# Values without their ones columns, loaded ahead of the second unit's queries and keys

## The chip, the cores and the metric

The kernel runs on one core of one Trainium2 chip. The metric is device time in microseconds (us); lower is better. Five engines take part: PE (TensorE, matrix products), DVE (VectorE), ACT (ScalarE), POOL (GpSimd) and SP (SyncE), which here only issues DMAs. Each runs its own queue strictly in order and meets the others at semaphores.

## The reference

The reference chains three layers. The change touches the first, a linear attention over 4 batches x 8 heads, 576 positions, head width 64, with 128 random features:

```python
q_p, k_p = (phi(q_s), phi(k_s))            # exp(projection - |x|^2/2 - max), 128 features
kv = np.einsum('bhsm,bhsd->bhmd', k_p, v)
z = np.sum(k_p, axis=2)
num = np.einsum('bhsm,bhmd->bhsd', q_p, kv)
den = np.einsum('bhsm,bhm->bhs', q_p, z)[..., None] + 1e-06
return (num / den).astype(np.float32)
```

A gated two-layer network of 2304 tokens (512 to 1536 to 512), the "MoE" of the code, and a soft mixture of 8 experts with 32 slots follow. Both are left as they are.

## The kernel before

**Units.** Attention goes in 16 units u of two heads each. A unit loads its transposed queries and keys (`QKTs`, from `qkT`), the same rows untransposed for the norms (`TOK`, from `tok`) and its values (`Vs`, from `von`). `chunk_proj` projects a piece of keys or queries on PE (K0, K1 and T for keys and tails, Q0 and Q1 for queries), DVE adds the norm and takes the minimum, ACT takes exponentials into `HKs`, `HTs` and `HQs`. `chunk_kv` multiplies the key features by the values, five matmuls for each head. `chunk_qT` transposes the query features, and `chunk_num` forms numerators and denominators, ACT and DVE divide, and the result goes into `XT`, the input of the next layer.

**The ones.** One matmul gives kv and z together: beside each 64 value columns stand 64 columns of ones (zero in the padded half of the fifth tile), values left for head 0 and right for head 1. Before, those constants lie in HBM inside `von` and come with each load: 640 KB per unit, 5120 contiguous bytes in each partition.

**Numerators in units 0 to 7.** There the numerator and the denominator of a half (288 positions) are four matmuls of 64 output rows, listed as `64x288`: denominator head 0, denominator head 1, numerator head 0, numerator head 1. Head 0 uses one half of the array's columns, head 1 the other.

**Order.** Nothing is written in program order. `Plan` records every operation with its reads and writes, a due time and a cost, `schedule` plays a list scheduler over all engines, and `issue` (L411) emits the result. For an overlap `span` takes the whole stretch from the first to the last element of an access, so a strided view stands for all that lies between. A change of one cost or dependency near the start can so reorder every engine for a long way. Matmuls of the MoE (`ga` gate, `va` value, `o` down) are due beside units 3 and on and fill PE. All of the trace's instructions carry line L411, so tiles tell them apart: `g_80` in an operand is `HKs`/`HQs`/`KVF` memory, `g1b` that of odd units, `g_78` the transposed inputs and `TOK`, `g_79` the values, `QTF` and the projection matrix.

Of the kernel before, what the change touches and what calls it, by code (L numbers as in the profile page):

```python
# [22 lines left out]
NT = 5  # L23
# [394 lines left out]
def body(ctx, tc, nc, qkT, tok, von, omT, wall, phi, w1, w2, ident_d, srep_d, rrep_d, mask_d, out):  # L418
    plan = Plan(nc)
    PE, ACT, DVE, POOL, SP = (Eng(plan, e) for e in ("PE", "ACT", "DVE", "POOL", "SP"))  # L420
# [54 lines left out]
    def region(k, dtype):  # L475
        return T([128, 4096], f"g{k}", dtype)
# [4 lines left out]
    def carve(reg, at, shape):  # L481
        n = int(np.prod(shape))
        names = "abcde"[:len(shape)]
        v = reg[:, at:at + n]
        if len(shape) == 1:
            return v
        return v.rearrange(f"p ({' '.join(names)}) -> p {' '.join(names)}",
                           **{c: d for c, d in zip(names, shape)})

    q0, q1, q2 = region(0, F32), half_region(0, F32), half_region(1, F32)  # L490
    g2, g3, g4 = (region(k, F32) for k in (2, 3, 4))
# [10 lines left out]

    QKTs = [carve(g2, 1152 * k, [1152]) for k in range(2)]
    TOK = carve(g2, 2304, [9, 2, D])
    Vs = [carve(g3, 1280 * k, [NT, 2, 128]) for k in range(2)]
    QTF = carve(g3, 2560, [2, S])
    obf = carve(g3, 3712, [256])
    HKs = [carve(r, 0, [4, 2, M]) for r in (g4, q2)]
# [17 lines left out]
    def bank(tag=None):  # L526
        if tag is None:
            tag = turn(FLW, "fl") if wide[0] else "fl"
        tag = "fl" if tag in POOLED else tag
        return plan.tile(psp, [128, 512], F32, tag, NFL if tag == "fl" else 1, dyn=tag == "fl")  # L530


    def load_unit(u):
        if u < NU:
            SP.dma_start(out=QKTs[u % 2], in_=qkT[u])
            SP.dma_start(out=Vs[u % 2], in_=von[u])
            SP.dma_start(out=TOK, in_=tok[u])

    def prep_qk(u, kind):
# [23 lines left out]
    def chunk_proj(u, i):  # L563

        if u >= NU:
            return
        c0, nt, hb, t0, g0 = PARTS[i]
        hb = hb[u % 2][:, t0:t0 + nt]
        x = QKTs[u % 2][:, c0:c0 + 128 * nt]
        if nt < 4:  # L570
            both = bank()[:, 0:256 * nt].rearrange("p (t h m) -> p t h m", h=2, m=M)
            ps = [both[:, :, h] for h in range(2)]
        else:
            ps = [bank()[:, 0:128 * nt].rearrange("p (t m) -> p t m", m=M) for _ in range(2)]

        def products():
            for t in range(nt):
                if nt < 4:
                    PE.matmul(both[:, t].rearrange("p h m -> p (h m)"), x[:, 128 * t:128 * t + 128], obf,
                              start=True, stop=True)  # L580
                    continue
                for h in range(2):
                    r = slice(64 * h, 64 * h + 64)
                    PE.matmul(ps[h][:, t], x[r, 128 * t:128 * t + 128], obf[r, 128 * h:128 * h + 128],
                              start=True, stop=True)

        plan.together(products, [SQ[:, g0:g0 + 2 * nt]], [hb])
        low = turn(MX, "mx")
        for h in range(2):
            for t in range(nt):  # L590
                g = 2 * t + h
                DVE.tensor_tensor_reduce(out=hb[:, t, h], in0=ps[h][:, t],
                                         in1=SQ[:, g0 + g:g0 + g + 1].to_broadcast([128, M]),
                                         scale=1.0 / 16.0, scalar=BIG, op0=ALU.add, op1=ALU.min,
                                         accum_out=low[:, g:g + 1])
        for h in range(2):
            for t in range(nt):
                g = 2 * t + h
                ACT.activation(out=hb[:, t, h], in_=hb[:, t, h], func=AF.Exp, scale=-1.0, bias=low[:, g:g + 1])

    def chunk_kv(u):

        ps = bank()[:, 0:256].rearrange("p (h c) -> p h c", h=2)
        for h in range(2):
            for t in range(NT):
                k = HKs[u % 2][:, t, h, :] if t < 4 else HTs[u % 2][:, 0, h, :]
                PE.matmul(ps[:, h, :], k, Vs[u % 2][:, t, h, :], start=t == 0, stop=t == NT - 1)
        if u < N_NUM:
            ACT.activation(out=KVF, in_=ps, func=AF.Copy, scale=1.0 / M)
            return  # L610
        ACT.activation(out=KV[:, 0], in_=ps, func=AF.Copy, scale=1.0 / M)
        DVE.scalar_tensor_tensor(out=KV[:, 1], in0=ps, scalar=1.0 / M, in1=KV[:, 0].bitcast(F32),
                                 op0=ALU.mult, op1=ALU.subtract)
# [552 lines left out]
    SP.dma_start(out=QKTs[0][:, 256:640], in_=qkT[0][:, 256:640])  # L1166
    SP.dma_start(out=QKTs[0][:, 640:1152], in_=qkT[0][:, 640:1152])
    SP.dma_start(out=TOK[:, 5:9], in_=tok[0][:, 5:9])
    SP.dma_start(out=QKTs[1], in_=qkT[1])
    SP.dma_start(out=Vs[0], in_=von[0])  # L1170
    SP.dma_start(out=ident, in_=ident_d)
    DVE.memset(one_b, 1.0)
    DVE.memset(den_b, 1e-6)
    DVE.tensor_scalar(out=obf, in0=obf, scalar1=-16.0 * float(D ** -0.25), scalar2=None, op0=ALU.mult)
# [4 lines left out]
    chunk_proj(0, "K1")  # L1179
    chunk_proj(0, "T")  # L1180
    SP.dma_start(out=TOK, in_=tok[1])
    SP.dma_start(out=Vs[1], in_=von[1])
    chunk_proj(0, "Q0")
    chunk_proj(0, "Q1")
    prep_qk(1, 0)
# [6 lines left out]
    start = START  # L1192
# [124 lines left out]
def layout(q, k, v, omega, moe_w_gate, moe_w_val, moe_w_out, moe2_phi, moe2_w1, moe2_w2):  # L1317
    def headsT(x):
        return x.reshape(B, H // 2, 2, S, D).transpose(0, 1, 2, 4, 3).reshape(NU, 128, S)

    def tiles(x, n):
        return x.reshape(NU, 2, n, 128, D).transpose(0, 3, 2, 1, 4)

    def pairs(x):
        return x.reshape(NU, 2, S, D)

    kT, qT = headsT(k), headsT(q)
    kp, qp, vp = pairs(k), pairs(q), pairs(v)
    tail = np.concatenate([kp[:, :, 512:], qp[:, :, 512:]], axis=2)
    vtail = tiles(np.concatenate([vp, np.zeros_like(vp[:, :, :64])], axis=2), NT)  # L1330
    ones = np.ones_like(vtail[:, :, :, 0])
    ones[:, 64:, NT - 1] = 0.0

    def up(w):
        return w.reshape(4, 128, NF, 128).transpose(2, 1, 0, 3).reshape(NF, 128, 512)

    f32 = np.float32
    p = np.arange(128)
    w2 = moe2_w2.reshape(E, 8, 128, DM).transpose(0, 2, 1, 3)
    big = np.finfo(f32).max  # L1340
    a = {
        "qkT": np.concatenate([kT, qT[:, :, 512:], qT[:, :, :512]], axis=2),
        "tok": np.concatenate([tiles(kp[:, :, :512], 4), tiles(tail, 1), tiles(qp[:, :, :512], 4)], axis=2),
        "von": np.stack([np.concatenate([vtail[:, :, :, 0], ones], axis=3),
                         np.concatenate([ones, vtail[:, :, :, 1]], axis=3)], axis=3),
        "omT": np.concatenate([omega.T, omega.T], axis=0),
        "wall": np.stack([up(moe_w_gate), up(moe_w_val), moe_w_out.reshape(NF, 128, DM)], axis=1).view(np.int64),
        "phi": moe2_phi.reshape(4, 128, NSLOT).transpose(1, 0, 2),
        "w1": moe2_w1.reshape(E, 4, 128, F).transpose(0, 2, 1, 3).reshape(E, 128, 4 * F),
        "w2": np.stack([x.reshape(E, 128, 2 * DM) for x in (w2[:, :, :4, :256], w2[:, :, 4:, :256],  # L1350
                                                            w2[:, :, :, 256:384], w2[:, :, :, 384:])], axis=1),
        "ident": np.eye(128, dtype=f32),
        "srep": (p[:, None] % 32 == np.arange(32)[None, :]).astype(f32),
        "rrep": (p[:, None] % 32 == p[None, :] % 32).astype(f32),
        "mask": np.where((p[:, None] % 32) // SPE == np.arange(E)[None, :], big, f32(0)).astype(f32),
    }
    return {f"in_{n}": np.ascontiguousarray(x) for n, x in a.items()}


def build(nc, arrays):  # L1360
    args = [nc.dram_tensor(n, a.shape, mybir.dt.from_np(a.dtype), kind="ExternalInput").ap()
            for n, a in arrays.items()]
    args.append(nc.dram_tensor("out_0", (NTOK, DM), F32, kind="ExternalOutput").ap())
    with tile.TileContext(nc, schedule_with_timeline_sim=True) as tc:
        with ExitStack() as ctx:
            body(ctx, tc, nc, *args)
# [8 lines left out]
```

## Time and profile before

| what | value |
|---|---|
| time, median of 3 runs | 684.1 us (683.9 to 684.46) |
| profiled execution, its own time | 683.73 us |
| span of that execution | 680.9 us |
| PE busy | 662.8 us |
| DVE, ACT, POOL busy | 442.4, 428.6, 283.7 us |
| DMA moved | 139.50 MB |

The span is what the trace shows of instructions; 2.83 us of the execution's own time lie outside it. Matmul ends are modelled and neighbours overlap in the trace, so the distance between starts tells more of PE than its busy time. An fp32 matmul has two records, an fp32r matmul or a transpose one.

### The profile page before, as it was taken

The page shows a single profiled execution, that of the slowest core. Times are in us where ns is not written, and L with a number is a line of the kernel's source. Part 1 is how long each engine was busy: PE and PEld are TensorE (multiplying, and loading weights), DVE is VectorE, ACT ScalarE, POOL GpSimd, SP SyncE. Part 2 cuts the span into 40 slices and gives each one's busy share as a digit, 9 for nine tenths or more (in the row PEclk, how much of TensorE's full clock was granted, in tenths as well). Part 3 has the DMA queues.
Part 4 walks back from the last instruction along what each step waited for, and adds up shares of the span by engine and source line. Part 5 has one row for each costly group of instructions (what it writes and reads, how often), then busy time and mean ns, then how long its engine had stood idle before and what let it go on. Part 6 is the DMA issues. An engine that isn't in the chain of part 4 may idle for free.

```text
span 680.9 us, 12655 instructions
## 1 busy us (share of the span) xinstructions
PE 662.8 (97%) x4404; PEld 534.2 (78%) x4404; DVE 442.4 (65%) x1306; ACT 428.6 (63%) x967; POOL 283.7 (42%) x245
## 2 busy tenths in 40 slices
PE   7999999999999999999999999999999999999995
PEld 6676777778888888887888888788888789899663
DVE  3899999899997476576566564566444335656423
ACT  5899898888887765756567675464444444675012
POOL 0465445465444443244444543444444444553100
PEclk9999999999999999999999999999999999999998
DMA  7889776787875345424353312689533238666988
GB/s 284 302 277 331 279 250 227 248 269 246 313 247 173 118 154 201 147 85 154 95 190 119 94 47 94 197 301 332 175 92 94 93 107 271 202 208 206 400 336 237
DMA packets 52494, 139.50 MB, mean 205 GB/s; under 512 B 5584, under 2 KB 13520, under 8 KB 52432
## 3 DMA queue, kind: packets, MB, share of 16 engines
q1 hardware_dynamic: 46624, 121.35, 53.0%
q10 hardware_dynamic: 5808, 17.37, 7.4%
q8 instruction: 34, 0.56, 0.3%
q14 instruction: 28, 0.23, 0.1%
HBM read 124.54 MB, written 14.16 MB: 204 GB/s over the span
## 4 chain that ended last, share of the span: by engine, by line
PE 86%; DMA 4%; DVE 3%; ACT 3%; issue 1%; SPq 1%; POOL 1%; DVEq 0%; POOLq 0%; ACTq 0%
PE o L411 25%; PE ga L411 22%; PE va L411 21%; PE fl L411 17%; DVE g L411 2%; DMA ws<-wscr 2%; ACT g L411 1%; DMA g<-in_von 1%; DMA g<-in_tok 1%; ACT ga_a L411 1%; SPq L411 1%; DMA wscr<-x 1%; DVE x2T L411 1%; POOL w L411 0%; POOL g L411 0%
## 5 line engine op out<-in xcount | busy, mean ns | idle before, releaser
L411 POOL TENSOR_TENSOR w<-ws,w 128x512 fp32r<-128x512 f32 x138 | 181.7, 1317 | 246.6 <-ACT w L411 114.3
L411 PE MATMUL ga<-XT,w 128*128 128x512 f32 (+1 forms) x720 | 168.4, 377 | 2.0 <-DVE ga_a L411 1.7
L411 PE MATMUL va<-XT,w 128*128 128x512 f32 (+1 forms) x720 | 167.3, 376 | 0.4 <-DVE ga_a L411 0.4
L411 PE MATMUL o<-gt,w 128*128 128x512 f32 (+1 forms) x720 | 167.5, 377 | 0.1
L411 PEld LDWEIGHTS ga<-XT,w 128*128 128x128 f32 x720 | 123.6, 189 | 27.2 <-DVE ga_a L411 2.6
L411 PEld LDWEIGHTS va<-XT,w 128*128 128x128 f32 x720 | 123.9, 189 | 25.9 <-issue 4.1
L411 PEld LDWEIGHTS o<-gt,w 128*128 128x128 f32 x720 | 123.6, 189 | 25.6 <-issue 3.9
L411 ACT ACTIVATE w<-ws 128x512 fp32r<-128x512 f32 x107 | 67.2, 628 | 61.1 <-PE o L411 19.5
L411 PE MATMUL fl<-g,g 64*128 64x128 f32 (+4 forms) x686 | 83.1, 313 | 3.2 <-DMA g<-in_qkT 1.4
L411 ACT ACTIVATE g<-g 128x128 f32<-128x128 f32 (+3 forms) x204 | 73.3, 410 | 13.9 <-DVE g L411 8.8
L411 ACT ACTIVATE ga_a<-ga_a 128x512 f32<-128x512 f32 (+1 forms) x120 | 69.9, 583 | 18.6 <-DVE ga_a L411 17.6
L411 PEld LDWEIGHTS fl<-g,g 64*128 64x128 f32 (+2 forms) x686 | 60.9, 183 | 23.7 <-issue 6.1
L411 ACT ACTIVATE ga_a<-ga 128x512 f32<-128x512 f32 (+1 forms) x60 | 33.2, 554 | 67.0 <-PE ga L411 66.9
L411 DVE SCALAR_TENSOR_TENSOR ga_a<-ga,ga_a 128x512 f32<-128x512 f32 (+1 forms) x60 | 38.0, 633 | 41.9 <-ACT ga_a L411 41.8
L411 DVE CAST w<-ws 128x512 fp32r<-128x512 f32 x55 | 23.5, 428 | 61.3 <-PE ga L411 41.6
L411 DVE TENSOR_TENSOR ga_a<-va,ga_a 128x512 f32<-128x512 f32 (+1 forms) x60 | 38.0, 634 | 17.7 <-ACT ga_a L411 12.5
L411 ACT ACTIVATE x2T<-g 128x512 f32<-128x512 f32 x72 | 45.4, 664 | 4.1 <-DVE x L411 4.1
L411 ACT ACTIVATE g1b<-g1b,g 128x128 f32<-128x128 f32 x128 | 40.4, 388 | 6.1 <-DVE g L411 6.1
L411 ACT ACTIVATE ga_a<-ga_a,one_b 128x512 f32<-128x512 f32 (+1 forms) x60 | 40.7, 679 | 1.4
L411 DVE TENSOR_SCALAR x2T<-x2T 128x512 f32<-128x512 f32 (+1 forms) x72 | 39.7, 564 | 2.8 <-ACT x2T L411 2.7
L411 DVE TENSOR_TENSOR g<-fl,g 64x288 f32<-64x288 f32 (+3 forms) x61 | 29.4, 484 | 17.8 <-ACT g L411 16.1
L411 POOL TENSOR_TENSOR XT<-g,XT 128x64 fp32r<-128x64 f32 (+2 forms) x43 | 28.6, 681 | 23.7 <-ACT ga_a L411 6.7
(197 smaller groups left out, 798.8 us busy)
## 6 DMA issues: line engine op xcount, KB each, us to landing
ws<-wscr SPq DMA_DIRECT2D x42, 512.0 KB, 3.6
ws<-wscr SPq DMA_DIRECT2D x78, 256.0 KB, 2.7
g<-in_wall SPq DMA_DIRECT2D x36, 512.0 KB, 4.9
g<-in_von SPq DMA_DIRECT2D x16, 640.0 KB, 5.7
wscr<-x SPq DMA_DIRECT2D x36, 256.0 KB, 4.8
g<-in_qkT SPq DMA_DIRECT2D x15, 576.0 KB, 5.1
g<-in_tok SPq DMA_DIRECT2D x15, 576.0 KB, 5.0
g<-in_w ACTq DMA_DIRECT2D x16, 512.0 KB, 5.5
```

What stands on the lines that cost most here:

```text
L411: ins = getattr(self.eng[e], method)(*a, **k)
```

## The change

The host layout drops the ones, so `von` holds 320 KB per unit, 2560 contiguous bytes per partition. In SBUF a unit's values are now three blocks of 5 x 64 columns: head 0, ones, head 1. The load writes blocks 0 and 2 (`0::2`, two runs of 1280 bytes in each partition), and DVE writes block 1 of both buffers once. The matmul of `chunk_kv` reads its 128 columns as two runs of 64, `h:h + 2`. The first value load now stands ahead of the second unit's `qkT`.

```diff
-    Vs = [carve(g3, 1280 * k, [NT, 2, 128]) for k in range(2)]
+    Vs = [carve(g3, 1280 * k, [3, NT, 64]) for k in range(2)]
...
-            SP.dma_start(out=Vs[u % 2], in_=von[u])
+            SP.dma_start(out=Vs[u % 2][:, 0::2], in_=von[u])
...
-                PE.matmul(ps[:, h, :], k, Vs[u % 2][:, t, h, :], start=t == 0, stop=t == NT - 1)
+                PE.matmul(ps[:, h, :].rearrange("p (a c) -> p a c", a=2), k, Vs[u % 2][:, h:h + 2, t, :],
+                          start=t == 0, stop=t == NT - 1)
...
+    SP.dma_start(out=Vs[0][:, 0::2], in_=von[0])
     SP.dma_start(out=QKTs[1], in_=qkT[1])
-    SP.dma_start(out=Vs[0], in_=von[0])
     SP.dma_start(out=ident, in_=ident_d)
+    for y in Vs:
+        DVE.memset(y[:, 1], 1.0)
+        DVE.memset(y[64:128, 1, NT - 1], 0.0)
...
-    SP.dma_start(out=Vs[1], in_=von[1])
+    SP.dma_start(out=Vs[1][:, 0::2], in_=von[1])
...
-        "von": np.stack([np.concatenate([vtail[:, :, :, 0], ones], axis=3),
-                         np.concatenate([ones, vtail[:, :, :, 1]], axis=3)], axis=3),
+        "von": vtail.transpose(0, 1, 3, 2, 4),
```

The scheduler turns this into another order on every engine. PE's order differs up to about a third of its list and is the same from there to the end. Three places follow.

PE, the first unit. Before, the two query projections of unit 0 (`fl<-g_79,g_78`, `o_87`) stand ahead of all ten kv matmuls (`o_88`):

```order
L411 MATMUL o_85<-g_79,g_78 128x256
L411 MATMUL fl<-g_79,g_78 128x256 x2
L411 MATMUL o_87<-g_79,g_78 128x256 x2
L411 MATMUL o_88<-g_79,g_80 128x128 x10
L411 MATMUL o_90<-ident,g_80 128x128 x4
```

In the changed kernel the same stretch reads:

```order
L411 MATMUL o_85<-g_79,g_78 128x256
L411 MATMUL o_88<-g_79,g_80 128x128 x5
L411 MATMUL fl<-g_79,g_78 128x256 x2
L411 MATMUL o_87<-g_79,g_78 128x256 x2
L411 MATMUL o_88<-g_79,g_80 128x128 x5
L411 MATMUL o_90<-ident,g_80 128x128 x4
```

Head 0's five kv matmuls, which need the values, moved ahead of the query projections, which do not.

PE, a little later: numerators of unit 0 (`64x288`) among projections of unit 1 (`128x256`). Before:

```order
L411 MATMUL fl<-g_79,g_80 64x288 x2
L411 MATMUL o_96<-g_79,g_80 64x288 x2
L411 MATMUL fl<-g_79,g_80 64x288 x2
L411 MATMUL fl<-g_79,g_78 128x256 x2
L411 MATMUL o_91<-g_79,g_78 128x256 x2
L411 MATMUL o_94<-g_79,g_78 128x256
L411 MATMUL o_100<-g_79,g_80 64x288 x2
```

In the changed kernel:

```order
L411 MATMUL fl<-g_79,g_80 64x288
L411 MATMUL o_96<-g_79,g_80 64x288
L411 MATMUL fl<-g_79,g_78 128x256 x2
L411 MATMUL o_91<-g_79,g_78 128x256 x2
L411 MATMUL o_94<-g_79,g_78 128x256
L411 MATMUL fl<-g_79,g_80 64x288
L411 MATMUL o_96<-g_79,g_80 64x288
L411 MATMUL fl<-g_79,g_80 64x288 x2
```

Head 0's denominator and numerator now stand alone ahead of the projections, and head 1's follow behind them; before, the two heads of each came together.

PE in unit 4, among MoE matmuls (`va`, `o` with `gt`, `ga`). Before:

```order
L411 MATMUL fl<-g_79,g_80 64x288 x4
L411 MATMUL va<-XT,w_152 128x512 x3
L411 MATMUL o_175<-gt,w_157 128x512
L411 MATMUL fl<-g_79,g_80 64x288 x2
L411 MATMUL o_175<-gt,w_157 128x512 x2
```

In the changed kernel:

```order
L411 MATMUL o_174<-gt,w_157 128x512 x2
L411 MATMUL fl<-g_79,g_80 64x288
L411 MATMUL o_174<-gt,w_157 128x512
L411 MATMUL o_175<-gt,w_157 128x512 x3
L411 MATMUL o_176<-gt,w_157 128x512 x3
L411 MATMUL fl<-g_79,g_80 64x288 x5
```

One matmul of a pair moved ahead of seven MoE matmuls, and the next five numerator and denominator matmuls stand together behind them.

## Rows read from the trace of the kernel before

**Rows 1.** Page, part 1: busy us (share of the span) and instructions of each engine.

```profile
PE 662.8 (97%) x4404; PEld 534.2 (78%) x4404; DVE 442.4 (65%) x1306; ACT 428.6 (63%) x967; POOL 283.7 (42%) x245
```

**Rows 2.** Chain of waits that ended last: start us, us, what it was.

```profile
4.53 0.43 SPq L411
...
5.00 0.43 SPq L411
...
5.48 7.99 DMA g<-in_von
...
13.60 2.92 PE o L411 x24
...
64.94 2.10 PE ga L411 x8
```

**Rows 3.** Windows: stretch, its length, engines' busy us (instructions), clock, DMA share, GB/s.

```profile
25.00:45.00 20.00, 18.37 (x118) 14.24 (x117) 19.05 (x89) 17.46 (x52) 12.69 (x13) 1.00 0.83 267
45.00:65.00 20.00, 18.78 (x134) 13.74 (x132) 18.67 (x77) 19.08 (x55) 10.79 (x12) 1.00 0.92 320
65.00:100.00 35.00, 35.00 (x220) 24.73 (x221) 33.41 (x108) 31.81 (x77) 15.40 (x14) 1.00 0.75 257
```

**Rows 4.** Timeline of PE, start: start us, us, operation, shapes, records [idle before].

```profile
7.34 2.77 PE L411 MATMUL o<-g,g 128*128 128x256 f32 x6
9.90 1.25 PE L411 MATMUL fl<-g,g 128*128 128x256 f32 x4
10.99 1.03 PE L411 MATMUL o<-g,g 128*128 128x256 f32 x4
13.60 2.47 PE L411 MATMUL o<-g,g 128*128 128x128 f32 x20 [1.58 <-DMA g<-in_von]
...
17.68 0.71 PE L411 MATMUL fl<-g,g 128*64 128x288 f32 x4 [0.52 <-ACT g L411]
18.22 0.66 PE L411 MATMUL o<-g,g 128*64 128x288 f32 x4
18.70 1.72 PE L411 MATMUL fl<-g,g 128*64 128x288 f32 x8
...
23.08 1.97 PE L411 MATMUL o<-g,g 128*128 128x256 f32 x8
24.88 0.61 PE L411 MATMUL fl<-g,g1b 128*128 128x128 f32 x4
```

**Rows 5.** DMAs issued from 4.6 to 7.5 us: count, size, us to landing.

```profile
g<-in_qkT SPq DMA_DIRECT2D x1, 576.0 KB, 6.9
g<-in_tok SPq DMA_DIRECT2D x1, 256.0 KB, 5.5
```

**Rows 6.** Timeline of DVE and ACT, 0 to 22 us.

```profile
0.86 0.64 DVE L411 MEMSET g<- 128x256 f32 x3 [0.86 <-PEq L1370]
...
9.63 1.86 ACT L411 ACTIVATE g<-g 128x128 f32<-128x128 f32 x6 [0.43 <-DVE g L411]
...
12.05 0.29 DVE L411 CUSTOM_DVE_ANT_0 g<-fl,g 128x128 f32<-128x128 f32 x1
...
12.39 2.45 ACT L411 ACTIVATE g<-g 128x128 f32<-128x128 f32 x8 [0.89 <-DVE g L411]
...
18.06 0.82 DVE L411 TENSOR_REDUCE g<-g 128x10 f32<-128x640 f32 x1 [4.23 <-POOL g L411]
...
21.17 0.28 DVE L411 CUSTOM_DVE_ANT_0 g1b<-fl,g 128x128 f32<-128x128 f32 x1
```

**Rows 7.** Timeline of PE, 50 to 81 us: numerators (128*64) among MoE matmuls.

```profile
53.04 0.70 PE L411 MATMUL o<-g,g 128*64 128x288 f32 x2
...
75.59 0.40 PE L411 MATMUL o<-gt,w 128*128 128x512 f32 x1
75.92 0.71 PE L411 MATMUL fl<-g,g 128*64 128x288 f32 x4
76.55 1.42 PE L411 MATMUL o<-gt,w 128*128 128x512 f32 x5
```

More of the change, by code (lines that the diff above doesn't have):

```diff
@@ L1330, in layout @@
     vtail = tiles(np.concatenate([vp, np.zeros_like(vp[:, :, :64])], axis=2), NT)
-    ones = np.ones_like(vtail[:, :, :, 0])
-    ones[:, 64:, NT - 1] = 0.0
     def up(w):
```

## The prediction

> **What bounds the kernel now.** I read the busy times first: PE is busy 97% of the span, DVE 65%, ACT 63% [rows 1]. So a change of loads pays only where PE waits for data. The chain of waits says where that is: it goes through the landing of the first values (7.99 us from issue, ending at 13.47), then PE at 13.60, then a mixture of engines until 64.94, and from there it is PE [rows 2]. The windows agree: from 65 to 100 us PE is busy 35.00 of 35, while in 25 to 45 and 45 to 65 it lacks 1.63 and 1.22 us, 2.85 in all, with DVE at 19.05 and 18.67 of 20 and ACT at 17.46 and 19.08 [rows 3]. Three stretches follow, each with its own price: the start up to 25 us, where PE waits for data; 25 to 65 us, where DVE, ACT and PE are all nearly full; and the rest, where every microsecond added to PE's list is a microsecond of the result and nothing that loads do matters.
>
> **The loads.** The queue of loads is served in order: the tokens issued at 4.53 land after 5.5 (10.0), the second unit's queries and keys, issued at 5.00, after 6.9 (11.9), the values at 13.47 [rows 2, 5]. The values thus take 1.6 us of the queue. The new load has half the bytes in twice as many runs. Its cost lies between 0.8 (by bytes) and 1.6 (no gain, the price of a whole load now); I take 0.9, near the bytes, because the runs are still above a kilobyte. It follows the tokens, so it lands at 10.9 (10.8 to 11.6), 2.6 earlier than before.
>
> **The start.** Were only the load moved, PE's wait of 1.58 us [rows 4] would go. But the scheduler moved head 0's kv matmuls ahead of the query projections, and PE takes its queue in order, so the projections now stand behind the wait for the values. Step by step. The T projection ends at 9.90. Head 0's kv matmuls start with the values at 11.0; their last one needs an exponential of T, and those end by 11.5 (9.63 + 1.86) [rows 6], in time. Twenty kv records took 2.47, so one head takes 1.1: until 12.1. The query projections are 8 records, 1.80 (23.08 to 24.88) [rows 4]: until 13.9. Head 1's kv: until 15.0. The query exponentials, which followed the first DVE operation by 0.34 (12.05 to 12.39) and take 2.45 [rows 6], now start at 13.4, half a microsecond behind the first projection's end at 13.0, and end at 15.85 instead of 14.84. The transposes wait for them and end at 16.1; the copies after them took 0.7 before the numerators at 17.68 [rows 4], so these start at 16.85. **Of 2.6 us in the load, 0.8 is left** at this place: the wait moved from the values to the exponentials.
>
> **The numerators.** Head 0 and head 1 use different halves of the array and run side by side. A pair, four records, takes one slot of 0.48 (18.22 to 18.70) [rows 4]. A lone matmul, two records, shows 0.70, a pair 0.71 [rows 7]: alone it costs the whole slot. Each group also costs its entry: a pair among MoE matmuls holds 0.63 (75.92 to 76.55), 0.15 over its slot, and starts 0.33 behind the record ahead of it, where five MoE records stand 0.25 apart [rows 7]; together 0.23. I counted both orders with the halves used: **40 slots against 34, 26 groups against 22**, so 6 x 0.48 + 4 x 0.23 = 3.8 us more work for PE. It falls on unit 0 with 2 slots and a group (1.2), units 1 to 3 with 3 slots and a group (1.7), units 4 to 7 with a slot and two groups (0.9).
>
> For unit 0 I lay it into the order: from 16.85 two slots and an entry (1.2) to 18.05, five projections (ten records, 2.2) to 20.25, three slots (1.7) to 21.95, a projection, a pair and a projection (0.9, 0.7, 0.9) to 24.45. Before, this point lay at 24.88, with four kv records (0.45) of the next unit already done: 24.43. **The lead on PE is nothing**, between 0.7 behind (values at 11.6) and 0.8 ahead (if the lone numerators hide).
>
> **25 to 65 us.** Units 1 to 3 bring 1.7 of array work. Against it stand shorter queues: five more value loads, each 0.7 shorter. PE lacks 2.85 us here, but DVE has only 2.28 idle (0.95 and 1.33) and ACT 3.46 [rows 3], so no more than 2.3 can be won. Between 0 and 2.3 I take 1.7: some lone matmuls were put in just where PE waited, and the projections of unit 1 start earlier. That covers the extra work exactly.
>
> **After 65 us** nothing covers 0.9. The later loads hang on no wait of PE [rows 3], and PE's order is the same in its last two thirds.
>
> **Small edits.** The four memsets cost about what three similar ones do, 0.64 [rows 6], doubled by size at most 1.3 on DVE: one pair lies in the idle start, the other among the T operations ahead of 11.0. If that cover fails, head 0's kv waits 0.4 more. The two-run read of the kv matmuls I cost at nothing; no row shows a moving operand in pieces. 320 records at 0.11 [rows 4] are 35 us, so a tenth more would be 3.5, a tenth less the same gain; I see no reason for either.
>
> **Sum.** 683.7 (the profiled execution) + 0.0 at the start + 1.7 - 1.7 + 0.9 = 684.6. The profiled execution lies 0.4 below the median of the runs, 684.1, so the forecast for the median is **685.0 us**. By about 0.2% (1.4 us) a measurement of this kernel can be told from no change: 685.0 is within it.
>
> **Rivals.**
> 1. *Slower: the lone numerators are not covered.* PE at 92 to 94% in 25 to 65 us speaks for it, and so do DVE and ACT, too full to move work ahead. The price is 1.7 + 0.9 = 2.6 over 684.1: 686.7. It decides once over 0.5 of the 1.7 shows; PE would then still lack about 2.9 us there.
> 2. *Faster: the vector side carries the lead.* DVE idles 4.23 us before 18.06, and its first operation on unit 1 starts at 21.17 [rows 6]. The projections of unit 1 now start at 18.05, so that operation could come at 18.65, 2.5 earlier. If units 1 to 3 are set by DVE and ACT, PE takes the extra slots in its waits, and one shorter load on the path gives 0.8: 684.1 - 2.5 - 0.8 + 0.9 = 681.7. Against it: at 24.45 PE has no lead, and it must do the same matmuls.
> 3. *Slower: the clock rises later.* Six records at 7.34 take 0.43 each (to 9.90), eight at 23.08 take 0.225, so PE runs at the lower level, 1.2 of 2.4 GHz, up to about 10 us, and rises while it works without a break [rows 4]. The new order puts an idle microsecond at 9.9, just there. If the rise slips behind the kv matmuls and projections, these cost 1.1 + 1.8 more: 685.0 + 2.9, less the 0.7 that the copies can take up, 687.2. The Trainium skill ("TensorE: Matmul & The Clock Gate", "Part 1: The HAM clock gate") states that the throttled clock is the default and that activity releases it. By that rule this rival is possible, and the rows agree with it so far as they go.
> 4. *The edit doesn't do what it says:* the loads are built as two runs each and 16 in number, so only their time is in doubt: at 1.6 each nothing is won by the queue, and the start loses 0.7: 685.7.
>
> **Chances.** Forecast 0.42, with its own range 683.2 to 685.5; rival 1 0.28; rival 2 0.20; rival 3 0.06; rival 4 and the two-run read 0.04. Faster by over 0.2%: 0.20; within: 0.42; slower: 0.38. The range for 8 in 10 takes in rival 1 and about half of rival 2, and leaves out rival 3: 681.9 to 687.0.
>
> **What would show it.** Right: the first kv record near 11.0 and then a wait for exponentials near 15.5; numerators near 16.9; the MoE records of unit 4 to 7 as dense as before and PE again without waits from 65 on; DMA bytes 5.2 MB lower (16 x 320 KB). Wrong: kv records that follow each other by more than 0.11, matmuls at 0.43 beyond 11 us, or MoE that is ahead by more than a microsecond at 65 us.

## The result, and the profile after

The changed kernel takes **691.7 us** (median of 5 runs, 689.6 to 693.4) against 684.0 for the kernel before beside it: ratio 1.0113, interval 1.0094 to 1.0133. It is slower by 1.1%, above the range of the forecast. On another chip, in a longer comparison (below), it took 688.5, ratio 1.0068 (1.0045 to 1.0091). Slower holds for both; the size is 0.7 to 1.1%. The profile below is of the fastest of the five runs (689.6). The five have mean granted TensorE clocks of 0.991 to 0.994 of full speed, the ten of the longer comparison 0.992 to 0.996, so a part of the distance between the two medians goes with the clock.

To see where the time went I use two marks that stand for exactly the same work in every kernel here. **M1** is the thirteenth gate matmul of the MoE: up to it each kernel has issued the same 340 matmul records on PE, all of units 0 to 3 and 24 of the MoE. **M2** is the first of the half-width gate matmuls of the last block; behind 230 us the orders of the two kernels are the same, so M2 stands for the same work too. Page, part 1, and the rows of the two marks, of the changed kernel; the columns are as in [rows 1, 4]:

```profile
PE 668.5 (97%) x4404; PEld 536.1 (78%) x4404; DVE 435.9 (63%) x1306; ACT 429.9 (63%) x970; POOL 282.4 (41%) x246
```

```profile
66.76 1.88 PE L411 MATMUL ga<-XT,w 128*128 128x512 f32 x7 [0.75 <-DVE ga_a L411]
...
568.69 1.60 PE L411 MATMUL ga<-XT,w 128*128 128x256 f32 x12
```

The same two marks in the kernel before: M1 is the row at 64.94 [rows 2], M2 this one:

```profile
564.47 1.60 PE L411 MATMUL ga<-XT,w 128*128 128x256 f32 x12
```

So the changed kernel is 1.82 us behind at M1, 4.22 at M2 and 6.2 at the end (spans 687.1 and 680.9). That is three losses of about 2 us: before 65 us, between 65 and 230 us, and after 570 us. The bytes fell by 5.24 MB, as they should; packets under 2 KB rose from 13520 to 17616.

The start, PE's timeline of the changed kernel, to set beside [rows 4]:

```profile
11.64 1.35 PE L411 MATMUL o<-g,g 128*128 128x128 f32 x10 [1.81 <-DVE g L411]
12.83 1.03 PE L411 MATMUL fl<-g,g 128*128 128x256 f32 x4
13.69 2.14 PE L411 MATMUL o<-g,g 128*128 128x256 f32 x14
15.67 0.60 PE L411 MATMUL o<-ident,g 128*128 128x128 f32 x4
...
17.74 0.70 PE L411 MATMUL fl<-g,g 128*64 128x288 f32 x2 [0.69 <-ACT g L411]
18.28 0.65 PE L411 MATMUL o<-g,g 128*64 128x288 f32 x2
...
22.81 2.83 PE L411 MATMUL o<-g,g 128*128 128x256 f32 x12
25.48 1.05 PE L411 MATMUL fl<-g,g1b 128*128 128x128 f32 x8
```

Head 0's kv matmuls stand alone at 11.64, ahead of the query projections at 12.83; the numerators at 17.74 are where they were before (17.68). The wait ahead of 11.64 is put down to DVE, but DVE's memset was over at 10.83 and the values landed at 11.5: issued at 5.01, 6.5 us to landing, 2.4 behind the tokens (4.53 and 4.6, so 9.1). DMA issues of that stretch, columns as in [rows 5]:

```profile
g<-in_von SPq DMA_DIRECT2D x1, 320.0 KB, 6.5
g<-in_tok SPq DMA_DIRECT2D x1, 256.0 KB, 4.6
```

The windows, columns as in [rows 3]:

```profile
25.00:45.00 20.00, 19.51 (x116) 14.64 (x116) 16.98 (x83) 18.57 (x56) 12.42 (x14) 1.00 0.77 247
45.00:65.00 20.00, 19.53 (x135) 14.46 (x134) 17.43 (x77) 18.70 (x55) 10.07 (x12) 1.00 0.89 302
65.00:100.00 35.00, 34.15 (x203) 24.42 (x202) 31.82 (x102) 31.20 (x75) 13.99 (x13) 1.00 0.64 223
```

These rows mislead whoever reads only PE. In 25 to 65 us PE is busier than before (39.04 against 37.15) and yet falls further behind: a numerator matmul that uses half the array counts as busy as a pair (put beside their partners in e3_paired, the same work keeps PE busy 37.64). DVE, the fullest engine of this stretch before, now idles 5.6 us of the 40 instead of 2.3.

### The profile page after: what moved, and what is told of

Read it like the earlier page. It is cut to its first block, busy times and chain, and to the rows that moved or that the text cites. A ratio compares the mean times of both kernels' runs of the same rounds, so it can differ in the third digit from the quotient of the medians.

```text
span 687.1 us, 12651 instructions
## 1 busy us (share of the span) xinstructions
PE 668.5 (97%) x4404; PEld 536.1 (78%) x4404; DVE 435.9 (63%) x1306; ACT 429.9 (63%) x970; POOL 282.4 (41%) x246
## 4 chain that ended last, share of the span: by engine, by line
PE 67%; ACT 2%; DMA 2%; DVE 1%; POOL 1%; issue 1%; DVEq 0%; POOLq 0%; ACTq 0%
PE o L411 21%; PE ga L411 18%; PE va L411 18%; PE fl L411 11%; DMA ws<-wscr 2%; ACT ga_a L411 1%; POOL w L411 1%; ACT g L411 1%; DVE ga_a L411 0%; ACT w L411 0%; DVE w L411 0%; DVE g L411 0%; DVE XT L411 0%; ACT XT L411 0%; DVE mx L411 0%
## 5 line engine op out<-in xcount | busy, mean ns | idle before, releaser
L411 POOL TENSOR_TENSOR w<-ws,w 128x512 fp32r<-128x512 f32 x141 | 184.2, 1308 | 254.0 <-ACT w L411 105.9
L411 ACT ACTIVATE w<-ws 128x512 fp32r<-128x512 f32 x104 | 65.4, 629 | 67.8 <-PE o L411 18.5
L411 PE MATMUL fl<-g,g 64*128 64x128 f32 (+4 forms) x686 | 85.8, 313 | 2.0 <-DVE g L411 1.1
L411 ACT ACTIVATE g<-g 128x128 f32<-128x128 f32 (+4 forms) x207 | 74.6, 414 | 16.3 <-DVE g L411 11.5
L411 DVE CUSTOM_DVE_ANT_0 g<-fl,g 128x128 f32<-128x128 f32 x142 | 32.6, 286 | 9.4 <-PE fl L411 9.3
```

What stands on the lines that cost most here:

```text
L411: ins = getattr(self.eng[e], method)(*a, **k)
```

## The experiments

The table gives, for each, the profiled execution's gap to the kernel before at M1, at M2 and at the end of the span (each the difference of the same two rows, or of the spans), then the median and the ratio with its interval. The medians of each kernel are compared with runs of the kernel before on its own chip; the gaps all go by one profile of the kernel before. How far they can be trusted shows where a kernel was profiled twice, or keeps the old order. At M1 two profiles of one kernel differ by 0.4 to 0.5, and e1_small_loads, in the old order, stands at -0.75 because its values landed 0.6 earlier (12.87 against 13.47). From M1 to M2 they differ by less than 0.1. A profiled execution need not be the median one: those of the changed kernel and of e9_before_to_65 are the fastest of their five and six.

| run | M1 | M2 | end | median us | ratio |
|---|---|---|---|---|---|
| changed kernel | +1.82 | +4.22 | +6.2 | 691.7 | 1.0113 (1.0094–1.0133) |
| e4_again | +1.43 | +3.88 | +3.7 | 688.5 | 1.0068 (1.0045–1.0091) |
| e1_small_loads | -0.75 | -0.74 | -1.0 | 682.7 | 0.9998 (0.9976–1.0020) |
| e2_new_order | +5.52 | +7.89 | +8.5 | 690.8 | 1.0107 (1.0074–1.0140) |
| e5_small_first | -2.18 | -2.15 | -2.8 | 681.2 | 0.9959 (0.9944–0.9973) |
| e12_small_first_again | -1.68 | -1.61 | -1.0 | 681.5 | 0.9975 (0.9964–0.9986) |
| e3_paired | +1.10 | +2.67 | +4.9 | 687.9 | 1.0060 (1.0041–1.0079) |
| e6_kv_back | +0.73 | +3.38 | +4.8 | 686.5 | 1.0032 (1.0014–1.0051) |
| e8_both | -0.13 | +1.78 | +3.0 | 688.4 | 1.0070 (1.0046–1.0093) |
| e13_start_mended | -0.27 | +1.85 | +2.0 | 685.1 | 1.0024 (1.0005–1.0042) |
| e7_start_before | +1.49 | +4.03 | +3.3 | 688.3 | 1.0069 (1.0044–1.0095) |
| e9_before_to_65 | +1.23 | +3.56 | +2.1 | 689.5 | 1.0096 (1.0066–1.0127) |
| e10_landing | +4.44 | +6.76 | +4.7 | 687.8 | 1.0069 (1.0054–1.0084) |
| e11_landing_late | +1.73 | +2.68 | +0.7 | 683.5 | 1.0001 (0.9989–1.0014) |
| e14_two_landings | +0.15 | +0.52 | -1.7 | 681.4 | 0.9977 (0.9963–0.9991) |

**Loads and order, one at a time.** The first pair takes the change apart. One kernel has the small loads and the constants written once, and keeps every engine's order of the kernel before; the other has the old loads and the new order. In both the planner is shown the other layout (`seen(a, b)`: issue a, plan with b); the first writes the constants on DVE right behind the small ones at its start.

```diff
-            SP.dma_start(out=Vs[u % 2][:, 0::2], in_=von[u])
+            SP.dma_start(out=seen(Vs[u % 2][:, 0::2], Vp[u % 2]), in_=von[u])
...
-    SP.dma_start(out=Vs[0][:, 0::2], in_=von[0])
     SP.dma_start(out=QKTs[1], in_=qkT[1])
+    SP.dma_start(out=seen(Vs[0][:, 0::2], Vp[0]), in_=von[0])
```

> New layout (loads of 320 KB in two runs, ones written once by DVE at the start, kv matmuls that read two runs), but every engine's instructions stand in the order of the kernel before; the first values stay behind the second unit's queries and keys. If the loss of 7.7 us comes from the new order, this is within 1.4 us of the kernel before, or up to 1.5 us faster by the shorter queue (682.5 to 685.4). If it comes from the small runs or from the read in two runs, it is slower by 4 us or more, and kv matmul records follow each other by more than 0.111 us.

```diff
-            SP.dma_start(out=Vs[u % 2], in_=von[u])
+            SP.dma_start(out=seen(Vs[u % 2], Vp[u % 2][:, 0::2]), in_=von[u])
...
+    SP.dma_start(out=seen(Vs[0], Vp[0][:, 0::2]), in_=von[0])
     SP.dma_start(out=QKTs[1], in_=qkT[1])
-    SP.dma_start(out=Vs[0], in_=von[0])
```

> Old layout (640 KB loads with the ones in them, one run per partition, kv matmuls that read one run, no memsets), but every engine's instructions in the order of the changed kernel, the first values ahead. If the order costs the time, this is near the changed kernel: 689.5 to 693.5, or 1 to 2 us more, because the first values are twice as large and head 0's kv waits for them. If the loads or the read cost it, it is near the kernel before, 683.5 to 686.

The small loads alone change nothing that the runs can tell (0.9998). The two-run read of the kv matmuls is free with them: the same 20 records take 2.47 as in [rows 4]. The new order with the old loads costs as much as the whole change, but not all of it is the order's. Its PE timeline shows one thing more:

```profile
12.48 2.48 PE L423 MATMUL o<-g,g 128*128 128x128 f32 x10 [3.24 <-DMA g<-in_von]
14.75 1.91 PE L423 MATMUL fl<-g,g 128*128 128x256 f32 x4
16.46 3.20 PE L423 MATMUL o<-g,g 128*128 128x256 f32 x14
19.49 0.60 PE L423 MATMUL o<-ident,g 128*128 128x128 f32 x4
```

From 12.48 to 19.49 lie 28 records that take 4.03 in the changed kernel (11.64 to 15.67) and 7.01 here. PE had idled 3.24 us for the larger load, and the window from 12 to 15 shows a granted clock of 0.50. This 2.98, and the kv matmuls' later start by 0.84, account for the difference of 3.7 at M1 between this kernel and the changed one. From M1 to M2, where no clock fell, it loses 2.37, as the changed kernel does (2.40).

**The changed kernel again**, on the chip of the pair above:

> The changed kernel once more, for a second trace. Its five times spread over 3.8 us (689.6 to 693.4), those of the kernel before over 0.9. Its first trace was of the fastest run and loses 1.8 us up to 65 us, 2.3 more up to 200 us and 1.7 between 575 and 590 us, where ACT waits 2.70 us for a reload of weights. If the spread comes from that late place, a slower trace has the same times up to 570 us and a longer wait there; if it comes from the start, the lag at 200 us differs from 4.1.

It is the reference for what follows: +1.43 at M1, +3.88 at M2. Its end shows how much of the spread lies after 570 us: from M2 on the changed kernel lost 2.0 in its first profile and won 0.2 in this one. There ACT rounds expert weights that come back from DRAM, in order, and PE waits for ACT's next copy. Timeline of ACT in the changed kernel, then in the second profile:

```profile
586.87 0.63 ACT L411 ACTIVATE w<-ws 128x512 fp32r<-128x512 f32 x1 [2.70 <-DMA ws<-wscr]
```

```profile
585.86 0.63 ACT L411 ACTIVATE w<-ws 128x512 fp32r<-128x512 f32 x1 [2.04 <-DMA ws<-wscr]
```

In the kernel before the same wait is 1.09. The longer wait alone does not make the 2.2 us. PE's timeline and one window (columns as in [rows 3]) of the first profile, then of the second:

```profile
588.04 0.33 PE L411 MATMUL fl<-ident,x2T 128*128 128x128 f32 x1 [1.64 <-ACT x L411]
...
590.46 2.77 PE L411 MATMUL o<-gt,w 128*128 128x256 f32 x12
590.00:594.00 4.00, 4.00 (x23) 4.00 (x22) 2.37 (x6) 1.70 (x4) 1.29 (x1) 0.57 0.50 153
```

```profile
587.03 0.33 PE L411 MATMUL fl<-ident,x2T 128*128 128x128 f32 x1 [0.98 <-ACT x L411]
...
589.34 1.60 PE L411 MATMUL o<-gt,w 128*128 128x256 f32 x12
590.00:594.00 4.00, 4.00 (x35) 4.00 (x35) 2.67 (x6) 2.66 (x7) 2.10 (x2) 1.00 0.42 134
```

PE waits 0.66 longer, and behind that wait its granted clock falls to half (0.57 in the mean of this window, 1.00 in the second profile): the next row follows the twelve records after 2.56 instead of 1.43. Laid record by record, the wait makes 0.7 of the difference and the clock 1.5. Four profiles have this fall at the same place, the changed kernel's, e3_paired, e6_kv_back and e8_both. They are the four in which PE waited longest for the copy there (1.16 to 1.64; at most 1.09 in the others), and each loses about 1.5 by it. Over all runs the stretch behind M2 gives between -2.2 and +2.2; I made no experiment on it, so why that reload comes early or late stays open.

**The old order with the values ahead.** This is the first kernel with one swap on SP; PE, ACT, DVE and POOL keep the order of the kernel before.

```diff
-        for _, i, (e, method, a, k) in self.schedule():
+        order = self.schedule()
...
+        order[v], order[q] = order[q], order[v]
```

> The kernel before in its order on every engine, with the smaller loads, the constants written at the start, and one swap on the SP queue: the first values ahead of the second unit's queries and keys. Theory 'the order of the compute engines costs it': as before or a little faster, 681.5 to 684.0 us, the first kv records at or before 13.5 us, the gap to the kernel before at 200 us between -1.0 and 0. Rival 'the move of the load costs it' (the second unit's queries and keys land 1 us later and its keys' projections wait): 684.5 to 687, the gap open by 25 us.

> The kernel before in its order, small loads, constants at the start, first values ahead of the second unit's queries and keys, once more on this chip: ratio 0.995 to 0.998, the gap to the kernel before -2.2 from 16 us to 570 us.

Faster than the kernel before, by 0.25 to 0.4%, on two chips. PE's timeline of the first of the two, with its marks:

```profile
10.12 3.57 PE L428 MATMUL o<-g,g 128*128 128x256 f32 x24
...
62.76 2.10 PE L428 MATMUL ga<-XT,w 128*128 128x512 f32 x8 [0.75 <-DVE ga_a L428]
...
562.32 1.59 PE L428 MATMUL ga<-XT,w 128*128 128x256 f32 x12
```

The second query projection and all 20 kv records run in one group without a wait, where the kernel before waited 1.58 at 13.60 [rows 4]. What is won here, 2.2, is won at M1 and at M2: nothing between takes it back. The second profile shows 1.7 and 1.6, less than the 2.2 expected. So the idea of the change is sound, and the order that came with it costs 3.1 to 4.0 at M1 and 5.5 to 6.4 at M2.

**Two places of that order on TensorE.** The lone numerators were put beside their partners; then head 0's five kv matmuls were put back behind the query projections; then both.

```diff
+        mine = [p for p, (_, i, (e, method, a, k)) in enumerate(order)
+                if e == "PE" and method == "matmul" and a[0].ap[0][1] == 64 and a[0].ap[1][1] == HALF]
...
+        order = [order[q] for p in range(len(order)) if p not in late
+                 for q in ([moved[p], p] if p in moved else [p])]
```

> The changed kernel with one thing undone: wherever the new order puts a numerator or denominator matmul of head 0 apart from its partner of head 1, it is issued right ahead of the partner again (33 slots of the array by my count of 34 before and 40 changed). If the lone matmuls cost what the prediction summed (6 slots and 4 groups, 3.8 us), this is 3 to 4 us under the changed kernel, 688 to 689. If they lie in waits of PE up to 65 us, only unit 4 shows, 0.5 to 1 us. If pairing delays the divisions of head 0 it can be slower than the changed kernel.

```diff
+        order = ([x for p, x in enumerate(order[:kv[5]]) if p not in kv[:5]] + [order[p] for p in kv[:5]]
+                 + order[kv[5]:])
```

> The changed kernel with one move on TensorE: the five matmuls of kv head 0 of unit 0 stand behind the four query projections again, just ahead of kv head 1. Theory 'they stood in front of the projections and waited for the values (11.64 us where 9.9 was to be had)': the query projections start near 10.0 instead of 12.8, the exponentials of the queries near 12.4, and the gap to the kernel before falls at 65 us from +1.4 to +1.8 to between -0.3 and +0.3, at 200 us from +3.8 to about +2.4; median 686.0 to 687.3. Rival 'the rest of the new order costs it, the start alone nothing': at 65 us still +1 or more, median 687.5 to 689.

> The changed kernel with both moves on TensorE: kv head 0 behind the query projections, and each lone numerator matmul beside its partner. If the two terms add (0.7 from the first and 0.8 to 1.2 from the second, as seen from 200 to 570 us): gap to the kernel before +2.0 to +2.6 at 200 us, median 685.5 to 686.5. If the rest of the order binds behind them (the ScalarE's casts of weights ahead of the unit-1 exponentials, which TensorE waited for at 20.9 us with the first move alone), one hides the other: gap +2.6 to +3.4, median 686.5 to 688.

Pairing gives 0.33 at M1 and 0.88 between M1 and M2 (2.45 less 1.57); with kv put back, 0.86 and 0.74. The figures between M1 and M2 are far above what two profiles of one kernel differ by; those at M1 are not, and the starts were not alike. PE's timeline with pairing alone:

```profile
11.00 2.48 PE L428 MATMUL o<-g,g 128*128 128x128 f32 x10 [1.25 <-DMA g<-in_von]
13.27 1.36 PE L428 MATMUL fl<-g,g 128*128 128x256 f32 x4
```

These kv records follow each other by 0.228, at half clock, behind an idle of only 1.25 us, and the transposes begin at 16.44 instead of 15.25 in the second profile of the changed kernel. By 25.2 us the paired kernel is only 0.16 behind it, and from there to M1 it wins 0.49. So up to M1 pairing is worth between 0.3 and 1.5 us, and these runs do not settle which.

The move of kv gives 0.70 at M1, not the 1.4 expected, though the numerators came 2.0 earlier than in the second run of the changed kernel (17.32), in part by luck: the query projections began at 8.99, where 10.0 was expected. PE's timeline and then ACT's with kv put back show where the rest went:

```profile
15.29 0.70 PE L416 MATMUL fl<-g,g 128*64 128x288 f32 x2 [0.69 <-ACT g L416]
...
20.89 0.71 PE L416 MATMUL fl<-g,g 128*64 128x288 f32 x4 [0.94 <-ACT g1b L416]
```

```profile
17.34 0.67 ACT L416 ACTIVATE x2T<-g 128x512 f32<-128x512 f32 x1 [2.10 <-DMA g<-in_wall]
```

With both moves PE waits 2.12 at 20.49:

```profile
20.49 0.71 PE L432 MATMUL fl<-g,g 128*64 128x288 f32 x4 [2.12 <-DVE g L432]
```

ACT stands at a cast of the first expert weights, which are not there yet, and the copies that free the numerators' bank stand behind it. In the old order these copies come first. The median with both moves, 688.4 (684.9 to 690.0), lies above what the marks say; four of its six runs are longer than the profiled one (686.7). They go with the granted clock: 684.9 at a mean of 0.997, 686.7 and 687.7 at 0.993 and 0.994, 689.1 to 690.0 at 0.991. Where the clock fell in the runs without a profile is not known.

**ScalarE's order.** So the next kernel has both moves, and on ACT the copies ahead of the second to fourth cast; unit 0's numerators stand ahead of unit 1's projections. Nothing else moves.

```diff
+FIRST = [
+    0, 1, 6, 8, 9, 10, 5, 11, 12, 7, 13, 2, 14, 20, 15, 16, 17, 22, 23, 3, 21, 55, 4, 24, 25, 26, 36, 27, 37,
...
+        order = [at[i] for i in FIRST] + [x for x in order if x[1] not in first]
```

> The changed kernel with three moves and nothing else: on TensorE kv head 0 stands behind the query projections and every numerator matmul beside its partner, those of unit 0 (three bundles) ahead of unit 1's projections; on ScalarE the copies that read unit 0's first numerators stand ahead of the second to fourth casts of the first expert weights, and two of these casts behind the first four exponentials of unit 1. DVE, GpSimd and the DMA queues keep the changed kernel's order. Theory 'TensorE lost the start to those casts, which wait for a weight load, and to the numerators that hold a PSUM bank behind them': no wait of TensorE over 1 us between 15 and 25 us (there was one of 2.1 with both TensorE moves alone), gap to the kernel before -2.5 to -1.0 at 65 us (-0.14 there) and -0.5 to +0.8 at 200 us (+1.8 there); median 682.5 to 684.5. Rival 'the vector engines as a whole, in the new order, are what binds': gap at 65 us -0.5 to +0.5, median 685 to 688.

The wait is gone: the longest wait of PE between 15 and 25 us is 0.69. But at M1 the gap is -0.27, as good as with the wait (-0.13):

```profile
21.37 1.97 PE L453 MATMUL o<-g,g 128*128 128x256 f32 x8 [0.69 <-DVE g L453]
...
64.67 1.88 PE L453 MATMUL ga<-XT,w 128*128 128x512 f32 x7 [0.75 <-DVE ga_a L453]
```

PE's waits between 15 and 30 us come to 2.5 in five pieces, for DVE, ACT and POOL, instead of 3.2 in three. The kv matmuls began 0.5 later in this run (11.85 against 11.33), so the move may be worth 0.6, not the 2 us that the one wait measured. My theory of the casts falls in its size; the rival, that the vector engines' order as a whole binds there, holds so far. Which part of it, these runs don't say.

**Cutting the two orders.** The first 153 operations (to about 24 us), and the first 503 (to about 65 us), in the order of the kernel before, the rest in the new one.

```diff
+        order = [at[i] for i in FIRST] + [x for x in order if x[1] not in first]
```

> The changed kernel's loads and constants; all engines follow the order of the kernel before in the first 153 operations (to about 24 us on TensorE), and behind that the order of the changed kernel. Theory 'the start costs 1.4, the stretch from 65 to 200 us costs 2.4': gap to the kernel before -0.6 to 0 at 24 us, within 0.5 of zero at 65 us, +2.0 to +2.6 at 200 us; median 685.7 to 686.7. Rival 'the losses behind the start are the start's own delay, passed on': the gap stays within 0.6 of zero to 570 us, median 683 to 684.5.

> As the run above, with the cut at 503 operations (about 65 us on TensorE): units 0 to 3 in the order of the kernel before, from the MoE's first blocks on the order of the changed kernel. Theory 'each stretch costs by itself': gap -0.7 to 0 at 65 us, then +2.4 between 65 and 200 us, so +1.7 to +2.4 from 200 on; median 685.2 to 686.5. Rival 'what is lost after 65 us comes from the late start': gap below +0.5 at 200 us, median 682.5 to 684.

With the old start the kernel is 0.6 ahead at 22 us and still 1.49 behind at M1. So the old start alone does not save M1. That the new order loses these 2 us between 24 and 65 us by itself is not shown: 119 records of the same work are done at 27.91 in the kernel before and at 29.53 here, so it is 1.6 behind within some six us of the cut, where the two orders are joined. The second cut certainly has such a seam, which spoils its M1:

```profile
61.17 0.73 PE L445 MATMUL ga<-XT,w 128*128 128x512 f32 x2 [2.54 <-POOL XT L445]
```

Up to 58 us it was 2.1 ahead. From M1 to M2 both lose 2.3 to 2.5, as the changed kernel does (2.4), whatever they had before. So the loss behind 65 us is not the late start passed on.

**What the planner believed.** The planner put kv first because by its rule the values land early: in its plan kv head 0 follows the T projection almost at once, in the two profiles of the changed kernel 0.8 and 1.8 us later. Three kernels tell it a later landing, for the first values by 1.7 or 2.5 us, or for them and the first expert weights by 1.7. (The condition on the time of issue takes in the values of units 0 and 1, both.) It makes the order by itself.

```diff
                         end = max(dma, now + nb / 340e3) + 2.0
+                        if ins and ins[0].tensor.name == "in_von" and now < 5.0:
+                            end += 1.7
```

> The changed kernel with one line in the planner: it takes the first values to land 1.7 us later than its own rule says, which is when they landed on the chip. By itself it then puts kv heads 0 and 1 behind the query projections, with 36 slots of numerators in 24 groups (34 in 21 for the kernel before, 41 in 25 for the changed one, counted alike). Theory 'the planner's early landing of the values is the cause': gap to the kernel before -2.2 to -1 at 25 us, within 1 of that at 200 us, median 681 to 683.5. Rival 'every new order is a draw of its own, and the tuned order of the kernel before a good one': a start as good, and +1 to +5 lost between 25 and 200 us, median 684 to 688.

> As the run above with 2.5 us instead of 1.7: the first 24 rows of TensorE are the same, the orders part behind them (36 slots in 22 groups). Theory 'landing': the same median as the run above within 1 us. Rival 'a draw': the gap at 200 us differs from that of the run above by more than 1 us.

> The changed kernel with the planner told that the first values and the first expert weights land 1.7 us later than by its own rule. It then puts kv behind the query projections and three of the four casts of the first expert weights behind the copies for the numerators, by itself; numerators 37 slots in 24 groups. Theory 'landings': gap to the kernel before -1.5 to 0 at 65 us, median 682 to 685. Rival 'every plan is a draw, and mended landings at two places do not steer the rest': gap anywhere from 0 to +5 at 65 us, median 684 to 688.

All three put kv behind the query projections. M1 of the three, in this order:

```profile
69.38 1.64 PE L413 MATMUL ga<-XT,w 128*128 128x512 f32 x6 [0.73 <-DVE ga_a L413]
```

```profile
66.67 2.98 PE L413 MATMUL ga<-XT,w 128*128 128x512 f32 x12
```

```profile
65.09 1.87 PE L413 MATMUL ga<-XT,w 128*128 128x512 f32 x7 [0.73 <-DVE ga_a L413]
```

A difference of 0.8 us in a believed landing moves M1 by 2.7 us and the median by 4.3. In the profiles of the first two, PE runs at half clock for a while behind a wait of 1.83 and 1.87 us for DVE (0.57 from 23 to 27 us in the first, 0.66 and 0.74 from 21 to 23 and 23 to 27 in the second); the third has no such fall, so some of its advantage at M1 is this. The first plan again has the weight cast early, and ACT waits there:

```profile
17.54 0.66 ACT L413 ACTIVATE x2T<-g 128x512 f32<-128x512 f32 x1 [2.65 <-DMA g<-in_wall]
```

With both landings mended that wait is gone, and the kernel is as fast as the best, 681.4. It does not settle that landings are the cause: at M1 it has no lead (+0.15, where -1.5 to 0 was expected), at M2 it is 0.5 behind, and its gain, 2.2, lies behind 570 us. That gain is not the scatter seen there in the other runs: all three planner kernels take 114.2 to 114.4 us from M2 to the end of the span, the other thirteen profiles 114.9 to 118.7. On DVE and ACT their order differs from that of the kernel before until some 593 to 599 us, and between 565 and 600 us PE has no wait over 0.16 in them; the kernel before has three there, 1.35 in all. For the values alone the theory has fallen (687.8, where 681 to 683.5 was expected). What stands, on four plans only (the changed kernel's and these three), is that a plan is close to a draw, over 4 us at M1, with the tuned order of the kernel before among the good ones.

## Why the prediction was wrong, step by step

1. *The loads.* The price was mis-sized here and too uniform. The values came 2.4 behind the tokens, not 0.9, and landed at 11.5, inside the bounds given (10.8 to 11.6). In ten other profiles with the values ahead of the second queries and keys they landed between 9.6 and 11.7. The issue itself takes SP 0.61 instead of 0.43.
2. *The start.* The chain was read rightly: kv ahead of the projections, the wait moved to the query exponentials. The point foreseen for 24.45 came at 25.48, 1.03 late. Of that, 0.64 is kv's start (11.64 for 11.0); 0.89 shows at the numerators (17.74 for 16.85). The sizes behind it hold: from the numerators to that point 7.6 foreseen, 7.74 measured. Even values at 9.6 would not have helped: in the second run of the changed kernel they landed then, and kv waited for the key exponentials until 11.22.
3. *The numerators.* Right in size where PE is the bound: 0.9 foreseen for units 4 to 7, 0.74 to 0.88 measured by pairing. For units 0 to 3, 2.9 was foreseen. Of this, 1.7 for units 1 to 3 is about right as work: from 25 to 65 us PE is busy 39.02 in the second profile of the changed kernel and 37.64 with pairing. But only 0.49 of it comes through as time; the rest returns as waits. What the 1.2 of unit 0 is worth is not settled, because PE's clock rose late in the paired profile.
4. *25 to 65 us.* Here the step failed on both sides. I let 1.7 us of shorter queues pay for 1.7 us of array work. From the point above to M1 0.77 was lost (1.05 to 1.82), though PE idled only 0.96 us of the 40 instead of 2.85; pairing, which takes the array work away, gives back at most a part of it. What else binds there was not found. And I capped what could be won at 2.3, by the idle time of a nearly full DVE. With the old order a start 2.2 earlier stays 2.2 earlier through the whole stretch in e5_small_first: an engine that is 95% busy within a shifted schedule is no cap, because all its work is shifted with it.
5. *After 65 us* 0.9 was foreseen, 2.4 came. What is missing, 1.5, was in the order listing: PE's order was said to be the same in its last two thirds, and so it is, but up to 230 us it differs in how the attention parts stand among the MoE. One piece is a wait for POOL, whose weight came late; five MoE records of 0.23 begin at 175.85, so the next one is 0.5 late:

```profile
175.85 1.41 PE L411 MATMUL o<-gt,w 128*128 128x512 f32 x5
177.52 2.60 PE L411 MATMUL va<-XT,w 128*128 128x512 f32 x10 [0.27 <-POOL w L411]
```

   The rest I found in no single place.
6. *After 570 us* I foresaw nothing, and the profile of the changed kernel lost 2.0 there, its repeat nothing. A longer wait for a reload and 1.5 us of half clock behind it make the difference.
7. *Rivals.* The first (lone numerators not covered, 686.7) had the right sign and a part of the cause: of its 2.6, pairing gives back 1.2 at M2 (3.88 less 2.67), and PE did not lack the 2.9 us in 25 to 65 that it named, but 0.96. The second (681.7) is what the change gives without its order, 681.2 and 681.5, though by another way than I put it: nothing was handed from PE to the vector side, the start was simply 2 us earlier for all. The third (the clock) did not come true at the start of the changed kernel, whose kv records at 11.64 follow each other by 0.12; it did in the kernel with the old loads and the new order, and its price there, 2.98, is the 2.9 that was worked out. It came true in e3_paired too, where these records follow each other by 0.228. By the Trainium skill ("TensorE: Matmul & The Clock Gate", "Part 1: The HAM clock gate") the low clock is the default and activity releases it. The granted clock of 0.50 behind the idle of 3.24 us agrees. But half clock behind 1.25 us in e3_paired and full clock behind 1.81 in the changed kernel show that the length of the idle alone does not decide.
8. *Memsets and two-run read* cost nothing, as said.

The steps that failed are the start's (values at 10.9, measured 11.5, and the numerators 0.89 late), the one that let 25 to 65 us come out at nothing (0.77 lost), and the 0.9 after 65 us (2.4). The forecast was wrong because it priced an order by the few places at which it could be laid beside the old one (start, pairs, groups) and set the rest at zero, for want of a reason in either direction. Of the 6.2 us at the end it had 0.9; the start's own step missed 1.0, and the places set at zero brought 0.8 up to M1, 1.5 up to M2 and 2.0 behind it, 1.5 of these by the clock of one profile. The median moved by 7.7, and no profile shows the rest: the profiled run is the fastest of the five.

## What to carry to other kernels

When a planner makes the order, a change of one load is two changes. Build the one with the old order held fixed (here 0.996 to 0.998 of the time before, against 1.007 to 1.011) before judging the idea, and treat a new order as a draw with a width of its own, which here is larger than what the load can win. Compare traces at marks that stand for the same work, not by busy shares: PE was busier by 1.9 us in the very stretch in which it fell behind. And look at the clock and at the start of each profile before you read half a microsecond out of two of them.

## What the runs showed of the hardware that I had not expected

- Behind an idle of 3.24 us ahead of its kv matmuls (e2_new_order) PE worked at half clock for some 6 us, nearly without a break; the windows of that kernel show it (columns as in [rows 3], the clock is the number behind the last bracket). An idle of 1.81 us at the same place in the changed kernel cost nothing, but one of 1.25 in e3_paired was followed by kv records at half clock.

```profile
12.00:15.00 3.00, 2.52 (x11) 2.55 (x12) 0.19 (x1) 0.00 (x0) 0.00 (x0) 0.50 1.07 385
15.00:18.00 3.00, 3.00 (x8) 2.37 (x8) 0.93 (x8) 0.96 (x4) 0.00 (x0) 0.50 0.95 372
18.00:21.00 3.00, 2.75 (x21) 2.42 (x20) 1.80 (x10) 2.08 (x8) 1.25 (x1) 0.90 1.04 378
```

- Shorter waits in the middle of the kernel were followed by a fall of the clock too: 1.16 to 1.64 us ahead of 590 us in four profiles, 1.83 and 1.87 ahead of 22 us in two. Others were not, 2.12 in e8_both and 2.54 in e9_before_to_65 among them, so the length of one wait does not tell.
- The first rise of the clock moves from run to run. The six records at 7.34 take 0.427 each [rows 4], twice the later 0.21; the same six in one of the planner's kernels take 0.22, though the column for the granted clock reads 1.00 there in both. The records show the level, the column does not show this first stretch.

```profile
6.69 1.48 PE L413 MATMUL o<-g,g 128*128 128x256 f32 x6
```

- The landing of one and the same load, at the same place in the queue, differs by 2 us between runs (9.6 to 11.7), as much as the load that the swap put behind it took of the queue (1.9, from 10.0 to 11.9).
- A load written as two runs of 1280 bytes per partition takes SP 0.61 us to issue at the start and 0.55 later, a load in one run 0.43 and 0.33.
